# Block 1 of a fused attention and MLP kernel: w4's decoding moved forward, w2's sums moved to other steps, two sums of w1 moved from TensorE to VectorE

## The chip, the cores and the metric

The kernel runs on one core of one Trainium2 chip. The metric is the device time of one execution in microseconds (us), lower being better. Times named below are from a hardware profile of one execution of the kernel before, or from its timed runs.

## What is computed

Inputs are q, k and v (8 batches, 8 heads, 576 positions, head dimension 64), two weights of a first MLP and two weights and a gain of a second one. In short:

```python
# chunked attention, 9 chunks of 64 positions
scores = (q_c @ k_c.T) / 8;  attn = softmax(scores);  x = attn @ v_c      # 4608 tokens x 512
# first MLP: w1 is 512 x 2048, w2 is 2048 x 512
h = x @ w1;  x = silu(h) @ w2
# second MLP: w3 is 512 x 1024, w4 is 1024 x 512
h = x @ w3;  e = exp(h - max(h));  solu = h * e / sum(e)
ln = (solu - mean) / sqrt(var + 1e-6) * g_ln
out = ln @ w4
```

## The kernel before

**Blocks and precision.** The 4608 tokens go through in 9 blocks of 512 (`BLK`), each of four tiles of 128 tokens. Every product is made from fp16 halves: an operand is split into a high and a low half, and high x high, high x low and low x high are added in PSUM, so a product costs three matmuls. A split is `split` (L115 on ScalarE writes the high half, L120 on VectorE the low one). Most instructions of both engines are splits and have these two lines, whatever the tile; the tile's name tells them apart: `w4h`/`w4l` is w4, `g` the activations after silu, `ws` a sum of weights on its way to DRAM, `vbh`/`vbl` v, `qbh`/`qbl` q, `kb` k, `x` the input of the next product.

**Weights.** Weights come from DRAM in 48 raw tiles of 512 KB (`wst`): 16 of w1, 16 of w2, 8 of w3, 8 of w4, in this order. Decoding one tile is three calls: `d1` (ScalarE, L136, `top<-wst`), `d2` (VectorE, L140, `wy<-wst,top`; it then fetches the next tile) and `d3`, the split (for w4 L115 writes `w4h`, L120 `w4l`). The decoding is spread over blocks 0 and 1; `NW1[f]` says how many decode steps follow group f in block 1, and the last tile to be decoded is the eighth of w4.

**The two forms of the first MLP.** Blocks 0 and 1 use the decoded weights as they are: `h_group(b, f)` (L419 to L421, 12 matmuls of 512 columns) for each of the 16 groups f of w1, then the products with w2 (L717 to L719, `x_ps<-g,w2t`). Blocks 2 to 8 use a form of a block product with seven half-size products in place of eight, which needs sums and differences of the quarters of w1 and w2. These are made once, in block 1: `w1_sums(p)`, eight of them, after groups f = `W1F`, and `w2_sums`, four of them, in steps s = `W2F`. Both end in DRAM (`w1s`, `w2s`) and are read back through a ring of buffers from block 2 on.

**One set of sums** (`pe_sums`, L437 to L463): each quarter is a high and a low half. TensorE joins halves by multiplying them with an identity (L448, `wq<-w,ident` or `wq<-w2t,ident`, two matmuls a quarter). ScalarE copies two joined quarters out of PSUM, y11 and y22 (L455, one copy for both with w1; L457 and L458 with w2), VectorE makes the four sums (L460 to L463), and each is split into a `ws` tile (L115, L120) and stored (L474).

**Block 1 in order.** After the scheduler's priorities, the order on TensorE is: the 16 groups, with the second MLP of block 0 between them: the first product and the softmax of tile n (`m_h`) before f = 5, 7, 9, 11 (`MHF`), the last product (`m_out`, L887 `o_ps<-w4h,uT`, L888 `o_ps<-w4l,uT`, L895) of two tiles before f = 13 and 15 (`MOF`), the third and the fourth behind the groups. `m_out` reads all eight tiles of w4. The softmax and layer norm behind `m_h` is a chain over VectorE and ScalarE: L742 (max), L836 (exponential, behind a load of its function table), L838, L844 (square), L854, L855, L858, and a DMA that transposes the result (`uT<-u`). Each of these chains waits for the transposes of the one before it, whose buffer it shares. Then come eight steps s of the product with w2 (24 matmuls of L717 to L719 in each), and with them the attention of block 2: scores of a tile at s = 0, 1, 3, 4 (`AT_S`; L227 to L229), its softmax (VectorE L231, L241, L243, L248 to L251, L254, ScalarE L242 or L238, L253), a DMA that transposes it (L256, `pT<-ae`) and `pv` (L273 to L275, `x_ps<-pT,vbh`) at s = 3, 4, 5, 6. Block 2 starts with `m_h` of block 1 (L736).

**Order and queues.** An engine runs its instructions in the order of its own queue. All DMAs named here are issued on SP's one queue. All PSUM tiles named here (`h_ps`, `wq`, `o_ps`, `s_ps`, `x_ps`) rotate through one set of eight banks, so a matmul into a bank waits for the last reader of the tile that was there before.

Of the kernel before, what the change touches and what calls it, by code (L numbers as in the profile page):

```python
# [13 lines left out]
AF = mybir.ActivationFunctionType  # L14
ALU = mybir.AluOpType
# [33 lines left out]
def fused(ctx: ExitStack, tc: tile.TileContext, qkv, w1, w2, w3, w4, g_ln, out):  # L49
    nc = tc.nc  # L50
    V, A, G, T = nc.vector, nc.scalar, nc.gpsimd, nc.tensor
# [8 lines left out]
    AT_S = (0, 1, 3, 4)  # L60
    NW0 = [2, 0, 0, 0, 3, 0, 2, 0, 1, 0, 3, 0, 1, 0, 3, 0]
    NX = [2, 2, 2, 2, 2, 2, 2, 0]
    NW1 = [2, 2, 1, 1, 1, 1, 1, 1, 1, 1, 1, 1, 1, 0, 0, 0]
    MHF = [5, 7, 9, 11]
    MOF = [13, 15]
    MO = (0, 1, 2, 3)
    W3S = [0, 3]
    W1F = [2, 4, 6, 8, 10, 12, 13, 14]
    W2F = [3, 1, 7, 3]
    EXB = [6, 7, 10, 13, 14]  # L70
    PHA = [8, 10, 11, 15, 32, 33, 34, 35]
    QF = 14
# [14 lines left out]
    for d in range(KD):  # L87
        for f in range(4):
            if f % 2 == 0:
                tag = f"w2_{2 * d + f // 2}" if d < 3 else f"q{12 + f // 2}"  # L90
                y = one.tile([P, 2, 2, 4, P], F16, tag=tag, name="w2t")
                w2t[d, f], w2t[d, f + 1] = y[:, 0], y[:, 1]

    w1s = [dram.tile([7, P, 2, 2, 2, P], F16, name=f"w1s{i}") for i in range(4)]
# [17 lines left out]
    def split(dst_h, dst_l, src, scale, eng_h, eng_l):  # L112

        if eng_h is A:
            ready[0] = A.activation(dst_h, src, AF.Copy, scale=scale).ins  # L115
        else:
            V.tensor_scalar(out=dst_h, in0=src, scalar1=scale, scalar2=None, op0=ALU.mult)
        if eng_l is G and scale == 1.0:
            return G.tensor_tensor(out=dst_l, in0=src, in1=dst_h, op=ALU.subtract).ins  # L119
        return V.scalar_tensor_tensor(out=dst_l, in0=src, scalar=scale, in1=dst_h,  # L120
                                      op0=ALU.mult, op1=ALU.subtract).ins
# [304 lines left out]
    def g_split(b, f, eng_h=V):  # L426
        return split(*g_of(b, f), graw.pop(f), S_G, eng_h, V)
# [3 lines left out]
    def flat(a, keep):  # L431

        if len(a.shape) == keep + 1:
            return a
        return a.rearrange("p l a b -> p l (a b)" if keep == 2 else "p a b -> p (a b)")

    def pe_sums(ys, quads, y1122=None):  # L437

        ys, quads = ([flat(a, k) for a in v] for v, k in ((ys, 1), (quads, 2)))
        n = 512 // quads[0].shape[2]  # L440

        def whole(qs):
            ps = [bank([P, n, 512 // n], "wq") for _ in range(len(qs) // n)]
            out = []
            for i, a in enumerate(qs):
                o = ps[i // n][:, i % n]
                for l in range(2):
                    T.matmul(o, ident16, a[:, l], start=l == 0, stop=l == 1)  # L448
                out.append(o)
            return ps, out  # L450

        y11, y12, y21, y22 = ys
        ps, o = whole([quads[0], quads[3]])
        if n == 2:
            A.activation(y1122, ps[0], AF.Copy)  # L455
        else:
            A.activation(y11, o[0], AF.Copy)  # L457
            A.activation(y22, o[1], AF.Copy)  # L458
        _, (p21, p12) = whole([quads[2], quads[1]])
        V.tensor_tensor(out=y22, in0=p21, in1=y22, op=ALU.add)  # L460
        V.tensor_tensor(out=y21, in0=y11, in1=p21, op=ALU.subtract)
        V.tensor_tensor(out=y11, in0=y22, in1=y11, op=ALU.subtract)
        V.tensor_tensor(out=y12, in0=p12, in1=y11, op=ALU.subtract)  # L463

    def sums(quads, dst, ys, staging, y1122=None):
        with tc.issue_after(last[0]):
            for j, a in ((0, quads[0]), (4, quads[1]), (6, quads[3])):
                nc.sync.dma_start(out=dst(j), in_=a)
        pe_sums(ys, quads, y1122)
        y11, y12, y21, y22 = ys  # L470
        for y, j in ((y11, 1), (y22, 2), (y21, 3), (y12, 5)):
            z = staging()
            split(z[:, 0], z[:, 1], y, 1.0, A, V)
            nc.sync.dma_start(out=dst(j), in_=z)  # L474
# [4 lines left out]
    def w1_sums(p):  # L479
        wa, wb = w1t[p], w1t[p + K1 // 2]  # L480
        y = one.tile([P, 4, 2, P], F32, tag=f"q{10 + p % 2}", name="y")

        def staging():
            sn[0] += 1
            return one.tile([P, 2, 2, P], F16, tag=f"xb{sn[0] % 3}", name="ws")

        sums((wa[:, :, 0:2], wa[:, :, 2:4], wb[:, :, 0:2], wb[:, :, 2:4]),
             lambda j: w1s[p // 2][j, :, p % 2], [y[:, i] for i in range(4)], staging,
             y[:, 0::3].rearrange("p n a b -> p n (a b)"))

    def w2_sums(c, q):
        ys = [one.tile([P, 2, 4, P], F32, tag=f"q{10 + i}", name="y") for i in range(2)]

        def staging():
            sn[0] += 1
            return one.tile([P, 2, 4, P], F16, tag=f"w1_{12 + sn[0] % 4}", name="ws")

        dst = w2s[2 * c + q]
        sums((w2t[c, q], w2t[c, 2 + q], w2t[2 + c, q], w2t[2 + c, 2 + q]),
             lambda j: dst[j], [ys[i // 2][:, i % 2] for i in range(4)], staging)  # L500
# [36 lines left out]
    def bank(shape, name):  # L537
        return ps1.tile(shape, F32, tag="mm", name=name)
# [210 lines left out]
    def w3_sums(k):  # L749

        if not w3s:
            for j, n in ((1, 0), (2, 1), (3, 2), (5, 3)):
                w3s[j] = one.tile([P, 2, 2, 512], F16, tag=f"w2_{n}", name="w3s")
            w3s[0], w3s[4], w3s[6] = w3q[0, 0], w3q[0, 1], w3q[1, 1]
        ys = [one.tile([P, 2, 512], F32, tag=f"w2_{4 + i}", name="y") for i in range(2)]
        y = [ys[i // 2][:, i % 2] for i in range(4)]
        pe_sums(y, [w3q[n, i][:, :, k] for n in range(2) for i in range(2)])
        for i, j in ((0, 1), (3, 2), (2, 3), (1, 5)):
            split(w3s[j][:, 0, k], w3s[j][:, 1, k], y[i], 1.0, A, G)
# [157 lines left out]
    for k in range(KD):  # L917
        for n in range(2):
            y = w3q[n, k // 2]
# [49 lines left out]
    def weights(n=1):  # L969
        for _ in range(n):  # L970
            d3()
            d1()
            d2()
# [35 lines left out]
    for b in range(NB):  # L1009
# [4 lines left out]
        for f in range(K1):  # L1014
            if b < FAST:
                if b == 1 and f in MHF:
                    n = MHF.index(f)
# [4 lines left out]
                if b == 0:  # L1022
                    weights(NW0[f])
                    if f:
                        g_split(b, f - 1, GH)
                else:
                    y = g_split(b, f, A)
                    with tc.high_priority(offset=-50), tc.issue_after(x_done[0]), tc.issue_after(x_done[1]), \
                            tc.issue_after(g_done[0]):
                        weights(NW1[f])  # L1030
                    with tc.high_priority(offset=1):
                        for p in range(8):
                            if W1F[p] == f:
                                w1_sums(p)
                    if f == QF:
                        load_qk(m, ("q8",))
                        with tc.issue_after(g_done[0]):
                            prep_qk(m, V, ahead=False)
# [19 lines left out]
        def step(s):  # L1058
# [36 lines left out]
            for n in range(4):  # L1095
                if b == 1 and W2F[n] == s:
                    w2_sums(n // 2, n % 2)
# [9 lines left out]
    b = NB - 1  # L1107
# [52 lines left out]
```

## Time and profile of the kernel before

| what | value |
|---|---|
| median of 3 timed runs | 1155.36 us (1153.68 to 1156.91) |
| the profiled execution's own time | 1155.39 us |
| its span in the trace | 1153.6 us |
| TensorE (PE) busy | 1120.0 us, 97% of the span |
| VectorE (DVE) busy | 898.9 us, 78% |
| ScalarE (ACT) busy | 803.2 us, 70% |

The profiled execution lies at the median; 1.8 us of its time are outside of the span. Block 1's groups run from about 121 to 205 us of the trace, its eight steps from 207.98 to 274.14 us. A row of the timeline gives the start, the duration, the engine, the line, the operation and its output and inputs, and in brackets how long the engine sat idle before it and who released it. Matmuls are pipelined: a row's duration holds the filling of the array too, and what one costs is the distance of starts.

### The profile page before, as it was taken

What the parts mean: (1) busy time and instruction counts of PE and PEld (TensorE: products, weight loads), DVE (VectorE), ACT (ScalarE), POOL (GpSimd) and SP (SyncE); (2) the same over time, 40 slices, a digit from 0 to 9 for tenths busy, and PEclk for the clock granted to TensorE, in tenths of its full rate; (3) what the DMA queues carried; (4) which work ended last, traced back from release to release, by engine and by line L of the source; (5) the groups of instructions that cost most, each with busy time, mean ns of one, the idle gap of its engine ahead of it and who ended that gap; (6) DMA issues with size and microseconds to landing.
All of it is one profiled execution on the core that took longest, in us unless ns stands there. A gap on an engine that the chain in (4) does not pass through costs nothing.

```text
span 1153.6 us, 23390 instructions
## 1 busy us (share of the span) xinstructions
PE 1120.0 (97%) x9036; PEld 765.8 (66%) x9036; DVE 898.9 (78%) x1654; ACT 803.2 (70%) x1456; POOL 137.0 (12%) x141
## 2 busy tenths in 40 slices
PE   7999997989999999999999999999999999999998
PEld 5444443445677776787578757875887678777853
DVE  6999797696868887888798888888889778886353
ACT  7997897564776787758775778477856875587253
POOL 3000000001003410121012101210031003100001
PEclk9999998999999999999999999999999999999999
DMA  8867779442565564885478548865776577465604
GB/s 306 277 182 222 219 186 263 148 153 82 156 191 176 175 162 136 210 237 157 137 212 226 172 122 225 230 171 131 201 232 172 154 192 236 140 165 160 202 15 118
DMA packets 205167, 209.15 MB, mean 181 GB/s; under 512 B 120192, under 2 KB 130432, under 8 KB 205056
## 3 DMA queue, kind: packets, MB, share of 16 engines
q1 hardware_dynamic: 205056, 207.66, 63.0%
q8 instruction: 70, 1.15, 0.4%
q14 instruction: 41, 0.34, 0.1%
HBM read 156.23 MB, written 24.12 MB: 156 GB/s over the span
## 4 chain that ended last, share of the span: by engine, by line
PE 60%; DVE 4%; ACT 4%; DMA 2%; issue 1%; POOL 0%; ACTq 0%; POOLq 0%
PE o_ps L895 4%; PE o_ps L888 4%; PE o_ps L887 4%; PE pa L655 4%; PE pa L657 4%; PE pa L656 4%; PE pa L548 3%; PE pa L550 3%; PE pa L549 3%; PE pa L782 2%; PE pa L780 2%; PE pa L781 2%; PE pb L548 1%; PE pb L550 1%; PE pb L549 1%; PE pb L655 1%
## 5 line engine op out<-in xcount | busy, mean ns | idle before, releaser
L115 ACT ACTIVATE q<-hc 128x512 f16<-128x512 f32 x196 | 120.5, 627 | 42.8 <-DVE hc L635 15.7
L120 DVE SCALAR_TENSOR_TENSOR q<-hc,q 128x512 f16<-128x512 f32 x196 | 138.2, 721 | 11.2 <-ACT q L115 9.0
L655 PE MATMUL pa<-q,ring 128*128 128x256 f16 x448 | 122.1, 273 | 0.0
L656 PE MATMUL pa<-q,ring 128*128 128x256 f16 x448 | 122.1, 273 | 0.0
L657 PE MATMUL pa<-q,ring 128*128 128x256 f16 x448 | 122.1, 273 | 0.0
L887 PE MATMUL o_ps<-w4h,uT 128*128 128x512 f16 x288 | 109.4, 380 | 7.2 <-ACT w4h L115 7.0
L888 PE MATMUL o_ps<-w4l,uT 128*128 128x512 f16 x288 | 109.4, 380 | 0.4 <-DVE w4l L120 0.4
L119 POOL TENSOR_TENSOR qbl<-qk,qbh 64x512 f16<-64x512 f32 x48 | 63.7, 1328 | 274.4 <-ACT qbh L115 218.0
L549 PEld LDWEIGHTS <-ring 128*128 128x128 f16 x784 | 76.7, 98 | 15.8 <-issue 5.5
L548 PEld LDWEIGHTS <-ring 128*128 128x128 f16 x784 | 76.7, 98 | 11.8 <-DMA ring<-w1s 1.4
L655 PEld LDWEIGHTS <-ring 128*128 128x128 f16 x784 | 76.7, 98 | 11.6 <-DMA ring<-w2s 0.6
L656 PEld LDWEIGHTS <-ring 128*128 128x128 f16 x784 | 76.7, 98 | 11.0
L657 PEld LDWEIGHTS <-ring 128*128 128x128 f16 x784 | 76.7, 98 | 8.9
L550 PEld LDWEIGHTS <-ring 128*128 128x128 f16 x784 | 76.7, 98 | 8.9
L851 POOL TENSOR_TENSOR c<-c,mhalf 128x2 f32<-128x2 f32 (+1 forms) x22 | 14.5, 661 | 546.3 <-DVE c L850 539.7
L895 PE MATMUL o_ps<-w4h,uT 128*128 128x512 f16 x288 | 71.6, 385 | 0.0
L548 PE MATMUL pa<-xb,ring 128*128 128x256 f16 x224 | 61.0, 272 | 2.7 <-DVE hc L606 2.7
L548 PE MATMUL pa<-x,ring 128*128 128x256 f16 x224 | 61.0, 272 | 1.2 <-ACT hc L573 0.5
L548 PE MATMUL pb<-x,ring 128*128 128x256 f16 x224 | 61.1, 273 | 1.1 <-DMA ring<-w1s 1.1
L655 PE MATMUL pb<-q,ring 128*128 128x256 f16 x224 | 61.1, 273 | 0.3 <-DMA ring<-w2s 0.3
L550 PE MATMUL pb<-x,ring 128*128 128x256 f16 x224 | 61.1, 273 | 0.0
L657 PE MATMUL pb<-q,ring 128*128 128x256 f16 x224 | 61.1, 273 | 0.0
(285 smaller groups left out, 3361.3 us busy)
## 6 DMA issues: line engine op xcount, KB each, us to landing
ring<-w1s SPq DMA_DIRECT2D x196, 256.0 KB, 3.3
ring<-w2s SPq DMA_DIRECT2D x196, 256.0 KB, 3.8
wst<-w SPq DMA_DIRECT2D x48, 511.8 KB, 4.7
qk<-qkv SPq DMA_DIRECT2D x29, 512.0 KB, 3.8
vs<-qkv SPq DMA_DIRECT2D x36, 256.0 KB, 2.9
out<-o SPq DMA_DIRECT2D x36, 256.0 KB, 2.3
w1s<-ws SPq DMA_DIRECT2D x32, 128.0 KB, 3.1
w2s<-ws SPq DMA_DIRECT2D x16, 256.0 KB, 2.0
```

Of the source, the lines that this page charges most:

```text
L115: ready[0] = A.activation(dst_h, src, AF.Copy, scale=scale).ins
L119: return G.tensor_tensor(out=dst_l, in0=src, in1=dst_h, op=ALU.subtract).ins
L120: return V.scalar_tensor_tensor(out=dst_l, in0=src, scalar=scale, in1=dst_h, op0=ALU.mult, op1=ALU.subtract).ins
L548: T.matmul(ps[:, c], wh, x[:, 0, k], start=first, stop=False, skip_group_check=True)
L549: T.matmul(ps[:, c], wh, x[:, 1, k], start=False, stop=False, skip_group_check=True)
L550: T.matmul(ps[:, c], wl, x[:, 0, k], start=False, stop=k == 1, skip_group_check=True)
L655: T.matmul(ps[:, c], wh, g[:, 0], start=first, stop=False, skip_group_check=True)
L656: T.matmul(ps[:, c], wh, g[:, 1], start=False, stop=False, skip_group_check=True)
L657: T.matmul(ps[:, c], wl, g[:, 0], start=False, stop=q == 1 and f == 3, skip_group_check=True)
L887: T.matmul(ps, uh[:, k], w4h[:, k, :], start=k == 0, stop=False)
L888: T.matmul(ps, uh[:, k], w4l[:, k, :], start=False, stop=False)
L895: T.matmul(ps, ul[:, k], w4h[:, k, :], start=False, stop=k == K2 - 1)
```

## The change

It has three parts. `NW1` moves decode steps of block 1 to earlier groups: f = 2, 3, 6 and 7 now have two, and the last is at f = 10 instead of f = 12. `W2F` moves the four `w2_sums` from the steps 3, 1, 7, 3 to the steps 5, 2, 7, 6, none of which is in `AT_S`. And in `pe_sums` for w1 (n = 2), y11 and y22 are no longer joined by four matmuls with the identity and one copy, but by two `tensor_tensor` additions on VectorE from the fp16 halves in SBUF; w2's sums (n = 1) are made as before. Over the program this takes 32 matmuls of 256 columns from TensorE and 8 copies from ScalarE and gives 16 additions of 128x256 to VectorE; the count of all else is unchanged. (From L456 on, line numbers of the changed kernel are one higher up to about L475.)

```diff
-    NW1 = [2, 2, 1, 1, 1, 1, 1, 1, 1, 1, 1, 1, 1, 0, 0, 0]
+    NW1 = [2, 2, 2, 2, 1, 1, 2, 2, 1, 1, 1, 0, 0, 0, 0, 0]
     MHF = [5, 7, 9, 11]
     MOF = [13, 15]
...
     W1F = [2, 4, 6, 8, 10, 12, 13, 14]
-    W2F = [3, 1, 7, 3]
+    W2F = [5, 2, 7, 6]
...
-    def pe_sums(ys, quads, y1122=None):
+    def pe_sums(ys, quads):
...
         y11, y12, y21, y22 = ys
-        ps, o = whole([quads[0], quads[3]])
         if n == 2:
-            A.activation(y1122, ps[0], AF.Copy)
+            for y, q in ((y11, quads[0]), (y22, quads[3])):
+                V.tensor_tensor(out=y, in0=q[:, 0], in1=q[:, 1], op=ALU.add)
         else:
+            _, o = whole([quads[0], quads[3]])
             A.activation(y11, o[0], AF.Copy)
             A.activation(y22, o[1], AF.Copy)
         _, (p21, p12) = whole([quads[2], quads[1]])
```

ScalarE's queue around the end of w4's decoding, near the first `m_out` of block 0. `w4h` is the high half of w4, `y<-wq` the copy of one set of w1's sums, `ws<-y` the split of a sum, `g<-g` the split of an activation, L423 the silu. Before:

```order
L836 ACTIVATE u,s<-h_ps,nm 128x512 x2
L115 ACTIVATE ws<-y 128x256 x3
L115 ACTIVATE w4h<-wy,gs 128x512
L844 ACTIVATE u,dv<-e,nmu 128x1024
L423 ACT_TABLE_LOAD
L423 ACTIVATE g<-h_ps 128x512
L115 ACTIVATE ws<-y 128x256
L855 ACTIVATE u<-e 128x1024
L115 ACTIVATE g<-g 128x512
L423 ACTIVATE g<-h_ps 128x512
L455 ACTIVATE y<-wq 128x2x256
L115 ACTIVATE g<-g 128x512
```

The L836 in it is the third softmax's, and the instructions that follow are the eighth `w4h`, a `ws` and the fourth softmax's L836. Now, from the second softmax's L844 on:

```order
L844 ACTIVATE u,dv<-e,nmu 128x1024
L115 ACTIVATE ws<-y 128x256 x2
L423 ACT_TABLE_LOAD
L423 ACTIVATE g<-h_ps 128x512
L855 ACTIVATE u<-e 128x1024
L115 ACTIVATE ws<-y 128x256
L115 ACTIVATE w4h<-wy,gs 128x512 x2
L115 ACTIVATE g<-g 128x512
L423 ACTIVATE g<-h_ps 128x512
L115 ACTIVATE g<-g 128x512
L836 ACT_TABLE_LOAD
```

The seventh and eighth `w4h` now stand ahead of the third softmax's L836; before, the eighth stood behind the third softmax's L855, one `ws` ahead of the fourth softmax's L836.

VectorE's queue at the same place, now, from the second softmax's L858 to the third's L838: L461 to L464 are the four sums of w1's fifth set (after f = 10), L455 is the first new addition of the sixth, `w4l` the low halves of w4.

```order
L858 TENSOR_TENSOR u<-e,u 128x1024
L120 SCALAR_TENSOR_TENSOR ws<-y,ws 128x256
L120 SCALAR_TENSOR_TENSOR w4l<-wy,gs,w4h 128x512 x2
L120 SCALAR_TENSOR_TENSOR g<-g 128x512 x2
L461 TENSOR_TENSOR y<-wq,y 128x256
L462 TENSOR_TENSOR y<-y,wq 128x256
L455 TENSOR_TENSOR y<-w_5_77 128x256
L463 TENSOR_TENSOR y<-y 128x256
L742 TENSOR_REDUCE mp<-h_ps 128x1
L464 TENSOR_TENSOR y<-wq,y 128x256
L838 SCALAR_TENSOR_TENSOR e,us<-h_ps,u 128x512
```

L464 is the last reader of its `wq` bank, and the first `m_out` takes that bank; it now stands behind L858 of the second softmax, two `w4l`, an L742 and an addition.

VectorE's queue in the steps, from the last scores' maximum (L231) on. Before:

```order
L231 TENSOR_REDUCE am<-s_ps 128x8
L462 TENSOR_TENSOR y<-y 128x512
L120 SCALAR_TENSOR_TENSOR ws<-y,ws 128x512
L463 TENSOR_TENSOR y<-wq,y 128x512
L120 SCALAR_TENSOR_TENSOR ws<-y,ws 128x512 x3
L241 TENSOR_TENSOR ae<-s_ps,am 128x512
L120 SCALAR_TENSOR_TENSOR vbl<-vs,vbh 64x8x64 x2
L243 TENSOR_REDUCE as<-ae 128x8
L396 TENSOR_TENSOR xd<-xf 128x256
L248 TENSOR_SCALAR as<-as 128x8
```

Now:

```order
L120 SCALAR_TENSOR_TENSOR x_1_2793<-x_ps,x_1_2793 128x512
L231 TENSOR_REDUCE am<-s_ps 128x8
L241 TENSOR_TENSOR ae<-s_ps,am 128x512
L120 SCALAR_TENSOR_TENSOR vbl<-vs,vbh 64x8x64 x2
L243 TENSOR_REDUCE as<-ae 128x8
L396 TENSOR_TENSOR xd<-xf 128x256
L248 TENSOR_SCALAR as<-as 128x8
```

The six instructions of w2's sums between L231 and L241 are gone from there; the sums of that set now stand behind this softmax.

## Rows read from the trace of the kernel before

**Rows 1.** The page, part 1: busy time, share of the span, instructions, by engine.

```profile
PE 1120.0 (97%) x9036; PEld 765.8 (66%) x9036; DVE 898.9 (78%) x1654; ACT 803.2 (70%) x1456; POOL 137.0 (12%) x141
```

**Rows 2.** Waits of PE, 113 to 285 us: us in total, times, longest us.

```profile
PE o_ps L887 <- ACT w4h L115: 7.0, 1, 7.0
PE x_ps L273 <- DMA pT<-ae: 3.4, 1, 3.4
PE x_ps L275 <- DVE vbl L120: 0.8, 1, 0.8
PE wq L448 <- ACT xf L379: 0.8, 1, 0.8
PE o_ps L888 <- DVE w4l L120: 0.4, 2, 0.2
```

**Rows 3.** Timeline of ACT, 178 to 189 us: start, duration, line, operation, [idle before].

```profile
179.69 0.42 ACT L115 ACTIVATE ws<-y 128x256 f16<-128x256 f32 x1 [2.72 <-DMA w1s<-ws]
...
182.95 0.72 ACT L115 ACTIVATE w4h<-wy,gs 128x512 f16<-128x512 f32 x1
...
186.60 0.69 ACT L836 ACTIVATE u<-h_ps,nm 128x512 f32<-128x512 f32 x1
```

**Rows 4.** Two stretches at the lower clock: bounds, length, busy us by engine, PEclk.

```profile
181.06:187.89 6.83, 3.96 (x10) 1.29 (x10) 5.42 (x10) 5.60 (x11) 0.00 (x0) 0.50 0.91 251
259.57:262.98 3.41, 3.09 (x29) 1.97 (x29) 1.06 (x4) 1.68 (x4) 1.65 (x3) 0.50 0.25 77
```

**Rows 5.** Timeline of PE around one set of w1's sums.

```profile
138.23 0.71 PE L448 MATMUL wq<-w,ident 128*128 128x256 f16 x5
138.78 1.03 PE L736 MATMUL h_ps<-w3q,x 128*128 128x512 f16 x4
```

**Rows 6.** Groups by line, 113 to 275 us: busy us, mean ns, idle.

```profile
L455 ACT ACTIVATE y<-wq 128x512 f32<-128x512 f32 x8 | 4.7, 589 | 0.0
...
L462 DVE TENSOR_TENSOR y<-y 128x256 f32<-128x256 f32 x8 | 3.4, 420 | 0.1
L460 DVE TENSOR_TENSOR y<-wq,y 128x256 f32<-128x256 f32 x8 | 3.3, 418 | 0.0
```

**Rows 7.** Busy time of the engines from 115.2 to 201.5 us.

```profile
115.20:201.50 86.30, 78.69 (x386) 37.98 (x385) 68.29 (x165) 73.34 (x133) 2.67 (x4) 0.96 0.81 222
```

**Rows 8.** Timeline of DVE behind the last scores.

```profile
246.62 0.68 DVE L231 TENSOR_REDUCE am<-s_ps 128x8 f32<-128x512 f32 x1
...
249.21 1.95 DVE L120 SCALAR_TENSOR_TENSOR ws<-y,ws 128x512 f16<-128x512 f32 x3
251.08 0.68 DVE L241 TENSOR_TENSOR ae<-s_ps,am 128x512 f32<-128x512 f32 x1
...
256.37 0.69 DVE L254 TENSOR_TENSOR ae<-ae 128x512 f16<-128x512 f32 x1
```

**Rows 9.** Timeline of PE at the first scores and at block 2.

```profile
207.98 0.19 PE L227 MATMUL s_ps<-kb,qbh 128*128 128x64 f16 x1
274.14 0.59 PE L736 MATMUL h_ps<-w3q,x 128*128 128x512 f16 x2
```

**Rows 10.** Timeline of DVE: the last operand of the first scores.

```profile
200.45 0.69 DVE L120 SCALAR_TENSOR_TENSOR kb<-qk,kb 128x512 f16<-128x512 f32 x1
```

**Rows 11.** L836 in block 1: xcount, ns min/median/max, first and last start us.

```profile
L836 ACT ACTIVATE u<-h_ps,nm x8: 677/683/691, 139.6 to 187.3; 128x512 f32<-128x512 f32 x8
```

**Rows 12.** PE's last m_h of block 0, and DVE's second softmax.

```profile
156.14 0.68 DVE L838 SCALAR_TENSOR_TENSOR e<-h_ps,u 128x512 f32<-128x512 f32 x1
161.25 1.03 PE L736 MATMUL h_ps<-w3q,x 128*128 128x512 f16 x4
```

**Rows 13.** DMA issues, 113 to 208 us: xcount, KB each, median us to landing.

```profile
wst<-w SPq DMA_DIRECT2D x9, 511.8 KB, 4.7
w1s<-ws SPq DMA_DIRECT2D x29, 128.0 KB, 3.4
```

**Rows 14.** Waits of ACT, 113 to 208 us.

```profile
ACT ws L115 <- DMA w1s<-ws: 10.7, 5, 4.1
```

## What was predicted, before the change was run

> **What bounds the kernel now.** I read the page's first part, then TensorE's (PE's) waits over the stretch the change touches. PE is busy 97% of the span [rows 1], so an edit pays only by taking PE work or PE waits away. Between 113 and 285 us PE waits in a few places [rows 2]: one wait of 7.0 us in `m_out` for `w4h`, with 0.4 us for `w4l` beside it, one of 3.4 us in `pv` for the transposed probabilities `pT`, and 0.8 us each for `vbl` and for the copy `xf`. Then I read the granted clock behind the long waits: it is 0.50, the lower of its two levels, from 181.06 to 187.89 and from 259.57 to 262.98 us [rows 4]. The engine had idled before each of these stretches, and the clock came back after it had worked again. PE is busy 3.96 and 3.09 us in them; at full clock that work takes half, so they cost 2.0 and 1.5 us more than the waits themselves.
>
> **Why PE waits for `w4h`.** ScalarE runs in order. At 179.69 it had sat 2.72 us for the store of an earlier sum, whose `ws` buffer it needed; behind that `ws` stood L855, a `g`, a silu, L455, another `g`, and only then the eighth `w4h`, at 182.95 [rows 3]. So the wait is a matter of place in the queue.
>
> **NW1.** It moves `w4h` and `w4l` two groups up, ahead of the third softmax's L836 instead of the fourth's. L836 runs in pairs from 139.6 to 187.3 us [rows 11], the fourth at 186.60 [rows 3], so they are about 15.7 us apart and the third pair was at about 171. The eighth `w4h` stands right in front of that pair's table load and a few instructions: done by about 167, with `w4l` one us later. PE, without waits, wants the first `w4l` of `m_out` at about 171 to 173: removed are 7.0 + 0.4 = 7.4 us, and the 2.0 us of slow clock with them. **Sum so far 9.4 us.**
>
> The moved calls take the same time as before. What they pass: the SP queue gets the 512 KB fetches earlier, among the `ws` stores, and they need 4.7 us to land where a store needs 3.4 [rows 13]; and the sums stand later on VectorE, since `w4l` goes first. The first `m_out` takes the bank whose last reader, L464 of the fifth set, now stands behind L858, two `w4l` and L742. By adding starts along VectorE's queue I put L464's end at 171.5 and PE at 170.5: a new wait of 1.0 us (0 to 3). The second `m_out`'s bank comes out free in time (0, or up to 1 if a store lands late). Behind the waiting matmul all of PE stands.
>
> **The additions on VectorE.** Removed from PE: 4 matmuls in each of 8 sets. Five of these matmuls start at 138.23 and what follows starts at 138.78 [rows 5], so one costs 0.11 us, and 32 cost 3.5 us, all on PE's path. **3.5 us gained.** ScalarE loses 8 copies of 0.59 us [rows 6], none of which PE waited for. VectorE gains 16 additions of 128x256 in f32. The rows have no addition from f16 in SBUF; the nearest are L462 (both inputs in SBUF) and L460 (one in PSUM), 420 and 418 ns [rows 6]. Below them I bound it at half and above at the same, and take 420 busy, about 0.34 us from start to start: 16 make 5.4 us (2.7 to 6.7). It is hidden as long as VectorE is not what ends last: from 115.2 to 201.5 us VectorE was busy 68.29 of 86.30 us, ScalarE 73.34 [rows 7]. After the change they need about 73.7 and 69 of some 81 us, so cover remains but 91% of an engine that runs in order is thin.
>
> The Trainium skill ("VectorE: DVE Perf Modes", section "Rules for kernel authors") says that chained VectorE operations are paid by their count; that speaks against this part, since it puts 16 more on the fuller engine, and it is the second rival below. The same page's section "The TRN2 errata" prices SBUF to SBUF at 58 cycles plus the elements and PSUM to SBUF at 120 plus the elements, 0.33 and 0.39 us here at 0.96 GHz; the rows show no such difference, 420 beside 418 ns, and by the table the 16 additions would cost VectorE an estimated 1.4 us less and PE nothing.
>
> **The first scores.** Block 1's gains until here are 7.4 + 2.0 + 3.5 = 12.9 us. PE began the scores at 207.98 [rows 9], so without new waits it is there at 195.1, and with the 1.0 at 196.1. The scores need `kb`'s low half from VectorE; before, it started at 200.45 and ended at 201.1 [rows 10], 6.9 us ahead of PE, so nothing waited. It stands behind the fourth softmax, and that chain is set by the one before it, not by PE: pairs of L836 are 15.7 us apart, and PE's first products 11 us. With `w4h` and L455 out of its way I put the fourth L836 at 185.5 instead of 186.6. Adding the starts of the 26 instructions between its L838 and `kb` (splits at 0.60, sums at 0.34, L858 at 1.14) gives 10.3 us, 0.7 before that: `kb` at 196.5, and 197.8 with one wait of VectorE for ScalarE in it. New wait 0.4 to 1.7, taken as 1.2; the upper bound is the old distance, 14.5 us from 186.6, or 201.1: a wait of 5. **New waits together 2.2 us (0 to 7).**
>
> **W2F.** Before, behind the last scores VectorE started L231 at 246.62, L241 at 251.08 and L254 at 256.37 [rows 8]; the `pT` transpose follows, and PE waited for it until 259.89, the 3.4 us. Between L231 and L241 stood six instructions of a set of w2's sums, 4.5 us by their starts (four of them `ws` low halves; the last three start at 249.21 [rows 8]), and the set delayed L231 too. Now the chain from scores to L254 is the softmax alone with a few splits: about 8.5 us instead of 13.5 from PE's scores. `pT` then lands about 2.9 us before PE wants it, and `pT` of the tile before 2.2 us ahead. `vbl` comes 1.6 us ahead for the same reason, and no sum takes a bank in the step where `xf` was waited for. Gone: 3.4 + 1.5 (clock) + 0.8 + 0.8 = 6.5 us. The sums themselves keep PE's work; they now lie in steps 2, 5, 6 and 7, the last as late as before, and beyond 274.14 (start of block 2, [rows 9]) nothing of them is awaited soon. **6.5 us gained (1.5 to 7).**
>
> **Sum.** 7.4 + 2.0 + 3.5 + 6.5 = 19.4 us less; new waits 2.2 us; net 17.2. Against the profiled execution's 1155.39 us, which is the median of the runs within 0.1 us, this gives 1138.2; I say **1138.0 us**.
>
> **Rivals.**
> 1. *The softmax chain sets the scores.* If VectorE and ScalarE stay as late as they were (fourth L836 at 186.6, `kb` at 201.1), PE waits 5 us at 196.1 and restarts at the lower clock, as after the 7.0 us wait, for about 1 to 2 us more. Of the 19.4 then 1.0 + 5.0 + 1.5 are lost: net 11.9, 1143.5 us. For it speak the 15.7 us period and 91% of VectorE; against it that the chain's waits for `w4h` and for stores fall away in part. Chance 0.2.
> 2. *A wait stays in part.* The last fetch of w4 or a `pT` comes late, and some 4 us of the 19.4 stay: 1142 us. `m_out` had 7.0 us to make up and has a margin of 5; `pT` had 3.4 and has 2 to 3. Chance 0.12.
> 3. *The stores starve ScalarE: slower.* ScalarE waited 10.7 us in five places for stores of w1's sums, none long enough to matter but one [rows 14]. The earlier 512 KB fetches land in 4.7 us each and stand on the same queue as the stores; the `ws` tiles rotate through three buffers, and `ws` stand directly ahead of L836. If each of the four chains starts 5 us later, its first products' banks are freed later: PE needed banks for the last `m_h` at 161.25 and the second softmax had read them by 156.8 [rows 12], a margin of 4.4, about 2.5 after the gains ahead of it. From there on PE waits one for one: 4 x 5.5 = 22 us against the 19.4 gained, some 1158 us. It decides from about 5 us a chain on; against it: the fetches are no more than before, only earlier, and four long waits would be needed where the trace has one. Chance 0.03.
> 4. *It does nothing.* The same order would come out of the scheduler; the queues of the changed kernel show that it does not. Chance 0.01.
>
> **How the numbers follow.** The forecast with 1134 to 1141 has 0.64. For all waits hidden and none new the time is 1136.0, and two us more if waits behind block 2's start fall away: 1134. The upper end takes in rivals 1 and 2: 1144.5. Outside lie rival 3 and 4 and tails of the others, about 0.15. This kernel's measurement can tell about 0.3%, 3.5 us, from no change: faster 0.96 (forecast, rivals 1 and 2), same 0.015, slower 0.025.
>
> **What the profile of after would show.** No wait of L887 for `w4h`, with PEclk 1.00 through the first two `m_out`: 9.4 us. No PE `wq<-w` matmuls but four a set: 3.5 us. No wait for `pT` after the last scores: 4.9 us. New rows to look for: PE waiting for VectorE's L464 at the first `m_out`, and for `kb`'s L120 at the first scores; if the latter is over 3 us, rival 1 holds. The first scores start at 196 to 198 us, block 2 at 256 to 258; behind that the two traces should run in parallel. The prediction is wrong if block 2 starts after 264 us, or if PE's idle time moves into the later blocks.

## The result, and the profile of the changed kernel

The changed kernel takes **1142.51 us** (median of 4 runs, 1141.74 to 1144.33) where the kernel before took 1154.95 in the same runs: a ratio of 0.9895, 95% interval 0.9883 to 0.9907, so about 12 us or 1.05% less. Forecast were 1138.0 with a range of 1134.0 to 1144.5: the direction and the range hold, the gain was forecast some 4.5 us too large. The profiled execution took 1141.74 us, span 1140.0; it is the fastest of the four.

Part 1 of its page (busy time, share of the span, instructions), to be held against [rows 1]:

```profile
PE 1112.4 (98%) x9004; PEld 760.5 (67%) x9004; DVE 904.2 (79%) x1670; ACT 798.8 (70%) x1448; POOL 137.0 (12%) x141
```

PE is busy 7.6 us less, with 32 matmuls less, and the span is 13.6 us shorter; VectorE (DVE) has 16 instructions and 5.3 us more, ScalarE (ACT) 8 instructions and 4.4 us less. PE's waits from 113 to 300 us, answering [rows 2]:

```profile
PE pa L548 <- ACT hc L566: 2.8, 1, 2.8
PE s_ps L228 <- DVE kb L120: 1.7, 1, 1.7
PE h_ps L736 <- ACT x L115: 1.5, 1, 1.5
PE pa L548 <- ACT hc L573: 0.5, 1, 0.5
PE x_ps L275 <- DVE vbl L120: 0.3, 1, 0.3
PE s_ps L227 <- ACT kb L115: 0.2, 1, 0.2
```

The 7.0 us for `w4h`, the 0.4 for `w4l`, the 3.4 for `pT` and the 0.8 for `xf` are gone. In their place stand four new ones: `kb` at the first scores (1.7 and 0.2), and, behind the start of block 2, `x` (1.5) and `hc` (2.8). The first was forecast, the other two were not.

**Up to the first scores** the forecast is met almost step by step. ScalarE's timeline has both last `w4h` at 162.12, ahead of the third L836, and the fourth pair of L836 from 183.97 where it was at 186.60 [rows 3]:

```profile
162.12 1.39 ACT L115 ACTIVATE w4h<-wy,gs 128x512 f16<-128x512 f32 x2 [0.20 <-DVE wy L140]
...
167.68 1.28 ACT L836 ACT_TABLE_LOAD   x1 [2.51 <-DMA uT<-u]
...
183.97 0.69 ACT L836 ACTIVATE u<-h_ps,nm 128x512 f32<-128x512 f32 x1
```

PE reaches the first scores after 13.2 us less than before (194.77 with 0.22 of wait in it, 207.98 in [rows 9]) and then waits for `kb`:

```profile
194.77 0.19 PE L227 MATMUL s_ps<-kb,qbh 128*128 128x64 f16 x1 [0.22 <-ACT kb L115]
196.62 0.21 PE L228 MATMUL s_ps<-kb,qbh 128*128 128x64 f16 x1 [1.67 <-DVE kb L120]
```

What was not in the sum is the clock behind that wait. Two stretches of the changed kernel, with PEclk in the column behind POOL: in the first PE worked all of 3.6 us at 0.53 of the clock, so nearly all of it at the lower level, which costs 1.7 us; the second is for later.

```profile
196.62:200.25 3.63, 3.62 (x30) 2.09 (x30) 3.17 (x8) 2.23 (x5) 0.00 (x0) 0.53 0.89 242
245.00:264.00 19.00, 17.54 (x82) 7.74 (x81) 18.40 (x32) 12.62 (x23) 1.11 (x1) 1.00 0.43 160
```

**The steps** take 61.24 us from 196.62 to the first matmul of block 2 at 257.86; without that clock and the 0.33 us for `vbl` they would take 59.2, against 66.16 before [rows 9]. Block 2 starts 16.3 us earlier than before, where 17.2 were forecast.

```profile
257.86 0.81 PE L736 MATMUL h_ps<-w3q,x 128*128 128x512 f16 x3
```

**Block 2 gives part of it back.** One of `m_h`'s products waits for the last split of `x`, and a product of block 2's first MLP for `hc` L566:

```profile
263.36 0.61 PE L736 MATMUL h_ps<-w3q,x 128*128 128x512 f16 x2 [1.46 <-ACT x L115]
...
279.52 0.27 PE L548 MATMUL pa<-x,ring 128*128 128x256 f16 x1 [2.75 <-ACT hc L566]
```

Of the 16.3 us gained at 257.86, 13.6 are left at the end of the span. The two new waits are 4.2 us, but others further on are gone (1.4 us for `ring` above all): from block 2's start to the end PE's waits sum to 7.9 us before and to 10.5 now. ScalarE's timeline there shows why the new ones came: the last split of `x` stands behind four `ws` of w2's last set, which follow VectorE one by one; then ScalarE waits 3.58 us for q and k of the next block (`qbh<-qk`), and behind these splits and that of `kb` stand L836 and, further on, the `hc` that PE waits for.

```profile
262.19 0.63 ACT L115 ACTIVATE ws<-y 128x512 f16<-128x512 f32 x1 [0.57 <-DVE y L464]
262.73 0.58 ACT L115 ACTIVATE x<-x_ps 128x512 f16<-128x512 f32 x1
266.89 1.28 ACT L115 ACTIVATE qbh<-qk 64x512 f16<-64x512 f32 x2 [3.58 <-DMA qk<-qkv]
268.20 0.63 ACT L115 ACTIVATE kb<-qk 128x512 f16<-128x512 f32 x1
270.81 0.69 ACT L836 ACTIVATE u<-h_ps,nm 128x512 f32<-128x512 f32 x1 [1.99 <-DVE nm L833]
```

ScalarE is not alone in this. The last 1.99 us of L836's wait are for VectorE: there the low half of `kb`, which waits for ScalarE's high half, stands ahead of the negated maximum (L833) that L836 needs.

```profile
268.86 1.67 DVE L120 SCALAR_TENSOR_TENSOR kb<-qk,kb 128x512 f16<-128x512 f32 x1 [2.92 <-ACT kb L115]
...
270.63 0.15 DVE L833 TENSOR_SCALAR nm<-mm__3222 128x1 f32<-128x1 f32 x1
```

And SP's queue shows why q and k are late: their loads (L173) are issued behind the four last stores of w2's sums (L475). The last row is from the kernel before.

```profile
260.38 3.51 SPq L475 DMA_DIRECT2D w2s<-ws  x4
263.99 0.91 SPq L173 DMA_DIRECT2D qk<-qkv  x2
...
274.65 0.95 SPq L173 DMA_DIRECT2D qk<-qkv  x2
```

In the kernel before, the same splits stood on ScalarE ahead of L836, but the loads were issued 0.5 us after block 2's first matmul (274.65 to 274.14); here they are issued 6.1 us after it. L836 ran 8.5 us after that matmul before (282.60 to 274.14) and runs 12.95 us after it now (270.81 to 257.86).

### The profile page after: what moved, and what is told of

The parts are those of the page before. It is cut to its first block, busy times and chain, and to the rows that moved or that the text cites. A ratio compares the mean times of both kernels' runs of the same rounds, so it can differ in the third digit from the quotient of the medians.

```text
span 1140.0 us, 23333 instructions
## 1 busy us (share of the span) xinstructions
PE 1112.4 (98%) x9004; PEld 760.5 (67%) x9004; DVE 904.2 (79%) x1670; ACT 798.8 (70%) x1448; POOL 137.0 (12%) x141
## 4 chain that ended last, share of the span: by engine, by line
PE 64%; ACT 4%; DVE 3%; issue 1%; POOL 0%; ACTq 0%; POOLq 0%
PE o_ps L895 5%; PE o_ps L888 5%; PE o_ps L887 5%; PE pa L655 4%; PE pa L657 4%; PE pa L656 4%; PE pa L548 3%; PE pa L550 3%; PE pa L549 3%; PE pa L782 2%; PE pa L780 2%; PE pa L781 2%; PE pb L657 2%; PE pb L655 2%; PE pb L656 2%; PE pb L548 2%
## 5 line engine op out<-in xcount | busy, mean ns | idle before, releaser
L548 PE MATMUL pa<-xb,ring 128*128 128x256 f16 x224 | 61.0, 273 | 3.1 <-DVE hc L606 3.1
L655 PE MATMUL pb<-q,ring 128*128 128x256 f16 x224 | 61.1, 273 | 0.0
L550 PE MATMUL pa<-xb,ring 128*128 128x256 f16 x224 | 61.1, 273 | 0.0
```

The source lines that it names most:

```text
L548: T.matmul(ps[:, c], wh, x[:, 0, k], start=first, stop=False, skip_group_check=True)
L550: T.matmul(ps[:, c], wl, x[:, 0, k], start=False, stop=k == 1, skip_group_check=True)
L655: T.matmul(ps[:, c], wh, g[:, 0], start=first, stop=False, skip_group_check=True)
```

## The experiments

Each edit is against the kernel named with it. Times are medians; the ratio is to the kernel before, run beside it, with its 95% interval. A difference of some 2 us between two rows is not clear of the noise unless their runs lie apart, as those of e_qk and the changed kernel do.

| run | what it is | us | ratio |
|---|---|---|---|
| p_nw1 | before + NW1 | 1151.6 | 0.9973 [0.9956, 0.9990] |
| p_w2f | before + W2F | 1151.8 | 0.9968 [0.9956, 0.9980] |
| p_add | before + additions on VectorE | 1149.2 | 0.9943 [0.9923, 0.9962] |
| u_add | NW1 + W2F | 1149.7 | 0.9960 [0.9947, 0.9972] |
| u_w2f | NW1 + additions | 1144.9 | 0.9911 [0.9888, 0.9935] |
| changed kernel | all three | 1142.5 | 0.9895 [0.9883, 0.9907] |
| e_2256 | changed, W2F 2, 2, 5, 6 | 1143.5 | 0.9905 [0.9890, 0.9920] |
| e_both | changed, W2F 2, 2, 5, 6 and QF 13 | 1142.3 | 0.9895 [0.9881, 0.9910] |
| e_qf13 | changed, QF 13 | 1141.7 | 0.9889 [0.9874, 0.9904] |
| e_qk | changed, q and k's splits behind the exponentials | 1140.1 | 0.9869 [0.9855, 0.9884] |
| e_g | changed, w2's low halves on GpSimd | 1146.7 | 0.9933 [0.9910, 0.9955] |
| e_gqk | e_qk + e_g + QF 13 | 1143.6 | 0.9901 [0.9881, 0.9921] |
| e_qkqf | e_qk + QF 13 | 1137.3 | 0.9865 [0.9843, 0.9886] |

The question after the result was where the last 4.5 us went. **Theory A**: W2F itself costs them, because two sets now stand in the last two steps. **Theory B**: block 2's start has a chain of its own that any earlier arrival uncovers.

### One part at a time: p_nw1, p_add, u_add

```diff
-    NW1 = [2, 2, 1, 1, 1, 1, 1, 1, 1, 1, 1, 1, 1, 0, 0, 0]
+    NW1 = [2, 2, 2, 2, 1, 1, 2, 2, 1, 1, 1, 0, 0, 0, 0, 0]
```

> The kernel before with the new NW1 alone. In the trace of the full change the wait for w4h is gone, and with it 7.4 us of waits and 2.0 us of slow clock. Theory A (the parts add up): the first scores start 9 to 10 us before 207.98, the steps keep their own waits of 0.8, 0.8 and 3.4 us with 1.5 of slow clock, block 2 starts at about 265, and the time falls by 8.5 to 10 us, to 1145 to 1146.5. Theory B (block 2 waits for qk and its first softmax whenever it is reached earlier, whatever moved): the time falls by only 5 to 6 us, to about 1149, with a wait of over 2 us for hc L566 behind block 2's start.

Measured: 1151.6 us (1148.8 to 1156.5 in 10 runs), a gain of 3.4 where 8.5 to 10 were expected. PE's waits in its profiled execution (which is its longest, 1156.51):

```profile
PE o_ps L887 <- DMA w1s<-ws: 2.9, 1, 2.9
PE h_ps L736 <- DVE y L463: 2.6, 1, 2.6
...
PE h_ps L419 <- ACT y L455: 0.8, 1, 0.8
```

The wait for `w4h` is gone, but PE now waits for a store ahead of `m_out` (2.9), for the bank that L463 reads (2.6) and for the copy L455 (0.8). So neither theory's size holds: in this execution NW1 alone replaces one wait by others in the same stretch. The hc wait that theory B expected did not come.

p_add makes the other half of that stretch alone:

```diff
-        ps, o = whole([quads[0], quads[3]])
         if n == 2:
-            A.activation(y1122, ps[0], AF.Copy)
+            for y, q in ((y11, quads[0]), (y22, quads[3])):
+                V.tensor_tensor(out=y, in0=q[:, 0], in1=q[:, 1], op=ALU.add)
...
```

> The kernel before with w1's y11 and y22 added on VectorE alone. PE loses 32 matmuls of 0.11 us. If all of PE's time is on the path: 3.5 us less, 1151 to 1152. If the w4h wait is set by ScalarE's queue (the rival: the wait ends when ScalarE ends, not when PE arrives), PE's earlier arrival only lengthens that wait, as far as ScalarE gains nothing from the removed copies: up to 2.5 of the 3.5 us are lost, 1153 to 1154.

Measured: 1149.2 us, 5.8 less: more than the 3.5 us of matmuls. In its profiled execution, which is its longest (1152.84 us), the wait for `w4h` is 2.2 us instead of 7.0, while those for `w4l` grew from 0.4 to 3.5:

```profile
PE o_ps L888 <- DVE w4l L120: 3.5, 2, 2.1
...
PE o_ps L887 <- ACT w4h L115: 2.2, 1, 2.2
```

u_add, NW1 and W2F together without the additions:

> The changed kernel with the additions undone: NW1 and W2F new, w1's y11 and y22 made by matmuls and a copy as before. Measured so far: the three parts alone give 3.1, 3.1 and 5.8 us by medians, all together 12.4, NW1 with the additions 10.1. Theory A (NW1 and the additions need each other: without them the sums' copies and banks on ScalarE and VectorE keep PE waiting where w4h did): NW1 and W2F together give only about 5 to 7 us, 1148 to 1150. Rival (the parts are worth the same in any company): 12.4 less 5.8, that is 6.6 us, no difference to see between the two; what tells them apart is the trace, by a wait of PE at 152 for L463 and at 192 for a store as NW1 alone has it (A), or none (rival).

Measured: 1149.7 us, inside both expectations; the trace, of an execution at the median, decides. PE waits 3.43 us for the copy L455 at a group's first matmul, 1.2 us for a store and 1.0 us for L463: the three waits of NW1 alone, in other sizes.

```profile
185.76 0.38 PE L419 MATMUL h_ps<-x,w 128*128 128x512 f16 x1 [3.43 <-ACT y L455]
```

So theory A's sign is there: with the sums made the old way, ScalarE's and VectorE's part of w1's sums (the copy, the bank's last reader, the `ws` behind the stores) is what PE meets once `w4h` is out of the way. The additions take a copy and a bank out of that chain. In time, though, no dependence between the parts shows: alone they are worth 3.4 (NW1), 5.8 (additions) and 3.1 us (W2F below), 12.3 in all, and together 12.4. With NW1 in the kernel and W2F as before, the additions are worth 6.7 us (1151.6 to 1144.9) instead of 5.8, and NW1 beside the additions 4.3 (1149.2 to 1144.9) instead of 3.4, which the spread of the runs doesn't tell apart. NW1 and the additions together give 10.1, where the forecast had 12.9 less 2.2. Why the additions bring more than PE's 3.5 us was not tested by itself.

In the changed kernel an addition costs what the bound above said. Groups by line (busy, mean ns, idle):

```profile
L455 DVE TENSOR_TENSOR y<-w 128x256 f32<-128x256 f16 x16 | 6.2, 416 | 0.0
...
L461 DVE TENSOR_TENSOR y<-wq,y 128x256 f32<-128x256 f32 x8 | 3.3, 417 | 0.0
```

With both inputs in SBUF L455 takes 416 ns, with one in PSUM L461 takes 417. The Trainium skill ("VectorE: DVE Perf Modes", section "The TRN2 errata") has two formulas: 58 cycles and the elements for SBUF to SBUF would be 327 ns, an estimate that this row rules out; its own measured form for an fp32 addition, 151 cycles and the elements, gives an estimated 424 ns, and with that the trace agrees.

### W2F alone and taken back: p_w2f, u_w2f

```diff
-    W2F = [3, 1, 7, 3]
+    W2F = [5, 2, 7, 6]
```

> The kernel before with the new W2F alone. The steps lose 6.5 us of waits and slow clock as forecast. Theory A (the sets in steps 6 and 7 hold back the last x split, the stores and behind them the load of qk): block 2 shows 1.5 us of wait for x and some 2.7 us for hc L566, so of 6.5 us about 3 stay: 1151.5 to 1153. Theory B (block 2's waits come from its earlier start): block 2 starts only 6.5 us earlier here, the new waits are under 2 us, and the time falls by about 5, to 1149.5 to 1150.5.

Measured: 1151.8 us, at the lower end of theory A's range. The rows are the first scores, the start of block 2 and the wait behind it:

```profile
208.85 0.19 PE L227 MATMUL s_ps<-kb,qbh 128*128 128x64 f16 x1
...
267.97 0.59 PE L736 MATMUL h_ps<-w3q,x 128*128 128x512 f16 x2
...
288.62 0.37 PE L548 MATMUL pa<-x,ring 128*128 128x256 f16 x1 [2.75 <-ACT hc L566]
```

The steps take 59.12 us instead of 66.16, so W2F does in the steps what it was forecast to do, 7.0 us; but the time falls by 3.1 only. The 2.75 us for `hc` is there although block 2 starts at 267.97, only 6 us earlier than in the kernel before: theory A's sign. (The wait for `x` is only 0.3 here, and the first scores start 0.9 us later than in the kernel before, 208.85 to 207.98.)

> The changed kernel with W2F back at 3, 1, 7, 3. Up to the first scores nothing changes: start at 194.8 with a wait of about 1.7 us for kb. Theory A: the steps' waits come back (about 5 us and 1.5 of slow clock), block 2's new waits of 1.5 and 2.75 us go: 1143 to 1145.5, 1 to 3 us slower than the changed kernel. Theory B: the steps' waits come back and block 2's stay in part: over 1146.

Measured: 1144.9 us, 2.4 more than the changed kernel; its four runs spread from 1143.2 to 1147.9, so this difference is not clear of the noise. The waits that tell, in its profiled execution, which is the longest of them:

```profile
PE x_ps L273 <- DMA pT<-ae: 3.4, 1, 3.4
...
PE o_ps L887 <- DVE y L464: 1.4, 1, 1.4
...
PE pa L548 <- ACT hc L566: 0.4, 1, 0.4
```

The steps' wait for `pT` is back; block 2's wait for `x` is gone, and that for `hc` has shrunk to 0.4, although block 2 starts at 268.2, when it does in p_w2f. Theory B falls: what makes the waits is not when block 2 starts, but where w2's sums stand. Note the 1.4 us for L464 at `m_out`: the wait that was forecast as 1.0 us. The changed kernel's profiled execution did not have it, and those of e_qk (1.7) and e_g (1.4), the same in block 1, did.

### Moving the sums elsewhere: e_2256, e_both

```diff
-    W2F = [5, 2, 7, 6]
+    W2F = [2, 2, 5, 6]
```

> The changed kernel with W2F at 2, 2, 5, 6: two sets in step 2, one each in 5 and 6, none in 7. Theory A (block 2's new waits come from the sets in the last two steps, whose stores stand ahead of qk's load on the queue and whose splits stand ahead of x's last split on ScalarE): the waits of 1.5 us for x and 2.75 us for hc L566 go or fall under 0.6 each, 3 to 4 us come off: 1138.5 to 1140. Theory B (block 2 is reached earlier, so its own chain is exposed): under 1 us of change.

Measured: 1143.5 us, no gain. Theory A was right on the waits and wrong on the time: block 2's waits for `x` and `hc` are both gone, but the steps have new ones (profiled in its longest execution, 1144.76):

```profile
PE s_ps L228 <- DVE kb L120: 4.6, 2, 3.0
PE x_ps L275 <- DVE vbl L120: 1.1, 1, 1.1
PE wq L448 <- ACT y L458: 0.6, 1, 0.6
```

Of the 4.6 us, 3.0 are for the `kb` of the fourth scores, and the clock was at its lower level behind them. The second row is a stretch that the changed kernel's fence above has too:

```profile
235.51:243.50 7.99, 6.92 (x60) 3.75 (x60) 6.84 (x13) 2.90 (x5) 1.28 (x2) 0.57 0.51 133
245.00:264.00 19.00, 19.00 (x131) 9.35 (x130) 17.51 (x32) 14.59 (x27) 2.58 (x3) 1.00 0.35 122
```

The steps last to 266.41, 68.8 us from the first scores. SP's queue shows the common element:

```profile
252.69 11.30 SPq L475 DMA_DIRECT2D w2s<-ws  x8
264.08 0.41 SPq L173 DMA_DIRECT2D qk<-qkv  x1
```

The last store of w2's sums is issued, and q and k's load behind it, at 264.08, in the changed kernel at 263.99. From 245 to 264 VectorE was busy 17.5 of 19 us here and 18.4 in the changed kernel. A reading that neither theory A nor B had is that VectorE is nearly full over the second half of the steps, so that the sets' place only decides whether PE meets its backlog before block 2 or behind its start. That is argued and not shown: the same time in these two runs may be chance, since e_both, with the same W2F, issues the load at 261.53, with VectorE busy 16.9 of the 19 us before, and VectorE was as full in the kernel before (18.8 of 19 us from 236 to 255). Shown is that the waits moved and the time did not.

> QF 13 and W2F 2, 2, 5, 6 together on the changed kernel. If both waits have the causes named and are apart in time, the gains add: 6 to 7 us off, 1135.5 to 1137. If PE's earlier arrival uncovers the next wait (pT or the ring), 1138 to 1140.

Measured: 1142.3 us, slower than either expectation. The gains don't add, since one of them is not there: the steps keep 4.2 us of waits for `kb`, 3.0 of them at the fourth scores.

### The first scores: e_qf13

```diff
-    QF = 14
+    QF = 13
```

> The changed kernel with QF 13 for 14: q and k of block 2's first tile are loaded and split a group earlier, so kb's low half stands ahead of the fourth softmax's L838 on VectorE instead of behind its L858. If the 1.9 us of wait at the first scores and the lower clock behind it (196.6 to 200, about 1.6 us) come from kb's place behind the softmax chain: both go, PE's first scores start at about 194.8 without a break, and 2.5 to 3.5 us come off the time: 1139 to 1140, unless the three splits and VectorE's three instructions delay the chain and that is waited for at the fourth tile. Rival (VectorE is full, whatever comes first): the wait moves to another matmul and the time stays within 1 us of 1142.5.

Measured: 1141.7 us, 0.8 less, which is within the noise, so the rival holds. The wait at the first scores is gone, as is the lower clock there; but 1.3 us for `kb` at the next scores, 2.0 for `vbl` and 1.1 for the copy L899 appear, and the `hc` wait is now the one with the lower clock behind it.

### The cause of the wait in block 2: e_qk

```diff
                     load_qk(m, ("w1_14", "w1_15"))
-                    prep_qk(m, ahead=False)
+                    with ExitStack() as behind_exps:
+                        if b == FAST:
+                            behind_exps.enter_context(tc.issue_after(exps[-1]))
+                        prep_qk(m, ahead=False)
```

> The changed kernel, but at block 2's start the splits of q and k of the next block (qbh, kb) come behind the first softmax's exponentials on ScalarE instead of ahead of them. In the changed kernel ScalarE waits there 3.6 us for qk, whose load was issued at 264 behind the last stores of w2's sums, and L836 starts at 270.8, 13 us after block 2's first matmul, where the kernel before needed 8.5. If this place in the queue is what makes PE wait 2.75 us for hc L566: that wait and the slow clock behind it go, 2.5 to 4 us off: 1138.5 to 1140. Rival (VectorE is what is late in the whole stretch; its sums end at 262 to 264 whatever the order): the softmax's VectorE part is late too, under 1.5 us off.

Measured: 1140.1 us (1139.7 to 1140.8), 2.4 less than the changed kernel, whose fastest run is 1141.74. The wait for `hc` is gone, the one for `x` has stayed:

```profile
PE o_ps L887 <- DVE y L464: 1.7, 1, 1.7
PE s_ps L228 <- DVE kb L120: 1.7, 1, 1.7
PE h_ps L736 <- ACT x L115: 1.5, 1, 1.5
```

L836 now follows block 2's first matmul (258.8) by 8.5 us, as in the kernel before:

```profile
267.27 0.69 ACT L836 ACTIVATE u<-h_ps,nm 128x512 f32<-128x512 f32 x1 [3.05 <-DVE nm L833]
```

The loads of q and k are as late as in the changed kernel (issued at 265.06, 6.3 us after block 2's first matmul). So the 2.75 us are shown to come from the splits of q and k that stand ahead of the softmax and wait for loads queued behind w2's stores: the high halves ahead of L836 on ScalarE, the low half of `kb` ahead of L833 on VectorE. The edit moved both, so the runs don't tell their shares. The 1.45 us for `x` are not touched by this edit; by the timeline shown above its split stands behind the four `ws`, but an edit that moves it ahead was not run.

### Taking work from VectorE: e_g, e_gqk

```diff
-            split(z[:, 0], z[:, 1], y, 1.0, A, V)
+            split(z[:, 0], z[:, 1], y, 1.0, A, eng_l)
```

In `sums`, `eng_l` is GpSimd for w2's sums and VectorE for w1's.

> The changed kernel with the low halves of w2's sums (16 instructions of 128x512) on GpSimd instead of VectorE. VectorE loses 16 x 0.60 = 9.6 us in the steps, GpSimd gains 16 of its own, 1.2 to 1.5 us each by the 64x512 and 128x256 rows it has. Theory C (the steps are filled by VectorE: the sums end at 262 to 264 in the changed kernel and with W2F 2, 2, 5, 6 alike): the waits for x (1.5 us) and hc L566 (2.75 us) shrink by at least half, 2 to 4 us off. Rival (the chain of stores and the qk load sets the end, and GpSimd is slower than VectorE): the stores end later, and the time is the same or up to 3 us longer.

Measured: 1146.7 us, 4.2 slower than the changed kernel: a miss, worse than its rival's 3. GpSimd's row (POOL), and SP's issue of q and k:

```profile
L119 POOL TENSOR_TENSOR ws<-y,ws 128x512 f16<-128x512 f32 x16 | 22.1, 1408 | 34.3 <-ACT ws L115 33.8 <-POOL ws L119 0.5
```

```profile
267.56 0.89 SPq L173 DMA_DIRECT2D qk<-qkv  x2
```

GpSimd needs 1408 ns for what VectorE does in 686 in the changed kernel, the stores on SP's queue wait 24.9 us in all for these low halves and ScalarE's copy L458 3.1 us, and q and k's load is issued at 267.56 instead of 263.99. PE waits 3.4 us for `x`. The 9.6 us taken from VectorE bought nothing: each sum still passes through the slower engine before its buffer is stored. This neither shows nor refutes a full VectorE; it fits the rival, that the chain of sum, split and store sets the end, with its slowest member.

> The two edits together (the splits of q and k behind the exponentials, w2's low halves on GpSimd) and QF 13. If the causes are apart: 1135 to 1138. If GpSimd's instructions delay the stores so that the ring or qk is late: 1140 to 1143.

Measured: 1143.6 us, just above the second expectation; the wait for `hc` is gone as in e_qk, that for `x` is 3.9.

### Two of the edits together: e_qkqf

> The changed kernel with QF 13 and the splits of q and k behind the exponentials at block 2's start. Alone they gave 1141.7 and 1140.1 us where the changed kernel has 1142.5. If the wait taken away at the first scores stays away (QF 13 moved 1.9 us of it, but vbl and a later tile's kb then waited 2.0 and 1.3): the gains add, 1139.0 to 1139.5. If VectorE takes it back in the same stretch: 1140, no different from the second edit alone.

Measured: 1137.3 us (four runs from 1136.97 to 1138.21, one of 1142.28), better than either expectation: by medians 5.2 us less than the changed kernel and 17.4 less than the kernel before. PE's waits from 113 to 300 us:

```profile
PE x_ps L275 <- DVE vbl L120: 2.0, 1, 2.0
PE s_ps L228 <- DVE kb L120: 1.2, 1, 1.2
PE o_ps L887 <- ACT o L899: 0.4, 1, 0.4
```

The 1.5 us for `x`, which the edits alone had left at 1.2 to 1.5, does not appear here. PE starts block 2 at 259.32, 1.5 us later than in the changed kernel, behind the 2.0 us for `vbl`, which has PEclk 0.60 behind it from 229.71 to 234; the split of `x` runs at 262.08 instead of 262.73. So PE meets this wait in the steps in place of block 2. Where the rest of the gain comes from is not shown, and the interval (0.9843 to 0.9886, with the run of 1142.28 us in it) overlaps that of e_qk, so it is not shown either that the two edits together beat e_qk.

## Why the prediction was right, and where its size was off

- **NW1, 9.4 us forecast.** The mechanism held: `w4h` was done at 163.5 and PE did not wait. The size of this term failed: alone it brought 3.4 us, beside the additions 4.3. The step that was wrong is "removed are 7.0 + 0.4" as the price of this part: without the additions PE meets the next waits of the same stretch (a store, L463, L455), and the prediction looked for the next wait only with all three parts in.
- **Additions, 3.5 us forecast.** Worth 5.8 alone and 6.7 with NW1. "ScalarE loses 8 copies, none of which PE waited for" was true of the trace and wrong as a price: with NW1 and without the additions PE does wait for that copy, 3.43 us in one place. The two errors cancel, which is luck: together the parts up to the first scores brought 10.1 us against 10.7 forecast. Only the joint sum was right; the split between its terms was not.
- **New waits, 2.2 us forecast.** `kb`: 1.9 measured, 1.2 forecast, upper bound 5. `m_out`'s bank: 0 in the profiled execution, 0.5 to 1.7 in those of other kernels with these parts, 1.0 forecast. Not in the forecast's sum was the lower clock behind the `kb` wait, 1.7 us; the prediction had it only in the first rival.
- **W2F, 6.5 us forecast.** The steps became 7.0 us shorter (p_w2f). The step that failed is the sentence that beyond the start of block 2 nothing of the sums is awaited soon. Something was: ScalarE's split of `x`, and SP's queue with the load of q and k. Measured worth of W2F: 3.1 us alone, 2.4 on top of the others. The prediction looked at the sums' own results and not at what stands behind their DMAs and splits on the queues, although with the change two of the four sets stand in the last two steps, where one stood.
- **The sum.** Block 2 starts 0.9 us later than forecast (257.86 against 274.14 less 17.2), 2.7 us are lost behind it, the median lies 0.8 above the profiled execution, and the forecast was put 0.2 below its own sum: some 4.5 us in all. One of the prediction's signs of being wrong came in part: PE's idle time did move into block 2, and behind its start the two traces do not run in parallel.
- **Rivals.** The first (the chain sets the scores) did not hold in its size: `kb` waited 1.9 and not 5. The second, a wait that stays in part, gave about the right time (1142 us) for the wrong reason: of the waits that were to go, only 0.3 us for `vbl` stayed. Stores that starve ScalarE (the third) were not seen: up to the first scores ScalarE waited 3.8 us for them in the changed kernel and 10.7 before [rows 14].
- What the Trainium skill says of counts of VectorE operations ("VectorE: DVE Perf Modes", section "Rules for kernel authors") did not decide here: 16 more cost VectorE 5.3 us busy, and p_add was faster by 5.8. The prediction calls this its second rival; the one that it bears on, with VectorE at 91%, is the first.

## To carry to other kernels

A wait removed from a full engine's path is worth at most the distance to the next wait in the same stretch: 9.4 us were read off the trace for one part, and 3.4 came of it alone. A right sum doesn't show that its terms are right; runs of one part at a time do. When work is moved later, read what stands behind it on every queue it uses, the DMA queue above all, up to the next stage that needs that queue: here q and k's load behind the last stores cost 2.75 us in another stage. Moving the sums within their stage moved the waits and not the time (e_2256, e_both); moving what needn't wait, the splits of q and k, out of the way is what helped (e_qk).

## What the hardware showed that I had not expected

The lower clock followed short waits in some executions and not in others. In the changed kernel PE waited 0.22 and 1.67 us at the first scores, and PEclk was 0.53 in the 3.6 us behind; in e_qk the same two waits (0.21 and 1.66) stand at the same place, and the stretch behind them is at full clock:

```profile
197.80:201.00 3.20, 3.20 (x35) 1.83 (x35) 2.96 (x7) 1.83 (x5) 0.00 (x0) 1.00 0.96 260
```

The same pair of waits had PEclk 0.57 behind it in u_w2f, and 1.00 in e_2256 and e_g. So a wait of this size may or may not cost as much again; what decides is not shown by these runs. GpSimd took 1408 ns for the low half of 128x512 that VectorE makes in 686.
